# A causal mask added in two row-tiled bf16 products for each head

## The chip, the cores and the metric

The kernel runs on one core of one Trainium2 chip. The metric is the device time of one execution in microseconds; the figure for a kernel is the median of its runs. A profiled execution is shown beside it: its span reaches from the first to the last instruction, and its time is a little longer than its span.

## The reference

Three parts follow each other. Causal attention over batch 2, 12 heads, 448 positions, head width 64; then two dense layers with a smooth step between them; then a gated pair and its output layer.

```python
scores = scale * np.matmul(q, k.transpose(0, 1, 3, 2))     # 2 x 12 x 448 x 448
mask = np.triu(np.ones((seq, seq), dtype=bool), k=1)
scores = np.where(mask, -1000000000.0, scores)
scores = scores - np.max(scores, axis=-1, keepdims=True)
attn = np.exp(scores)
attn = attn / (np.sum(attn, axis=-1, keepdims=True) + 1e-09)
out = np.matmul(attn, v)                                    # then (896, 768)
...
h = x @ w_in                                                # (896, 2048)
g = np.where(h >= 1, h, np.where(h <= -1, 0.0, (h + 1) ** 2 / 4))
x = g @ w_out                                               # (896, 768)
...
g = x @ w_gate; val = x @ w_val                             # (896, 1536)
return (g / (1 + np.exp(-g)) * val) @ w_out2                # (896, 768)
```

## The kernel before, in words

Attention works on pairs of heads. A tile `qk_t` holds the transposed queries and keys of two heads, the first in partitions 0 to 63, the second in 64 to 127. The 896 tokens are handled in two groups of 448: group 0 is the first 224 positions of both batches, group 1 the last 224. There are 12 units (a batch and a pair of heads) in each group. A unit of group 0 is one step (`j == 0`, query blocks 0 and 1 of 112 rows each), a unit of group 1 is two steps (`j == 2` and `j == 3`, one query block each): 12 + 24 = 36 steps. `SEGS` says for each step which stretches of columns its scores have: 112 and 224 columns, or 336, or 448.

A step goes through the engines like this. `scores` puts the products of queries and keys into the PSUM tile `s`, one bank for each head (TensorE, line 249); each is fp32 and runs in two passes, and its operands are the 64 rows of one head. Behind it the same function adds the causal mask to the last 112 columns of each stretch, by a product of a bf16 identity with a bf16 mask, 112 rows each (line 255). `greatest` reduces to the row maximum (VectorE, lines 267 and 269), `exps` takes the exponential (ScalarE, line 281), `normalize` divides by the sum (VectorE, lines 292, 293, 305), `turn` transposes the weights (TensorE, line 316), `turned` copies them out of PSUM (ScalarE, line 325), and `values` multiplies with the values (TensorE, line 336 for group 0, 349 for group 1), whose outputs for the two heads stand in the two halves of the columns. `x_hi` and `x_lo` split the result for the next layer.

The steps are pipelined: one pass of the main loop holds the scores of step k + 1, the normalization of step k, the transposes of step k - 1 and the values of step k - 2, in an order that the lists in `ORDER` give. That order is what the program states; when it is built, a scheduler puts each engine's instructions in the order in which they are expected to be ready, the stated order deciding between those that are. So scores, transposes and values of neighbouring steps can be interleaved otherwise than stated.

Where TensorE would have nothing to do, the loop gives it filling work: up to the second step of group 1 products of zeros (`zeros`, line 370, bf16, 512 columns; 18 ahead of everything as a warm-up, then `HOLD` many in each step), later the products of the first dense layer (`h_products`, lines 70 to 72). The weights of that layer arrive meanwhile, and VectorE unpacks them (lines 108, 115, 119, 128). Nine of sixteen blocks of the layer are done for group 0 during attention; all else of the dense layers follows.

The constants are made at the start: `ident` by GpSimd, `mask_b` by a memset on VectorE (line 374) and a selection on GpSimd (line 378), `ident_b` by one copy on VectorE (line 382).

Of the kernel before, what the change touches and what calls it, by code (L numbers as in the profile page):

```python
# [8 lines left out]
F32 = mybir.dt.float32  # L9
# [4 lines left out]
ALU = mybir.AluOpType  # L14
# [3 lines left out]
B, H, S, D = 2, 12, 448, 64  # L18
# [3 lines left out]
C = 112  # L22
# [14 lines left out]
MASK = -1.0e9 * 8.0  # L37
BF16 = mybir.dt.bfloat16
LOW_V = 9
NORM_P = 0  # L40

ORDER = {
    0: "copy scores max fill values x_hi weights norm x_lo turn exp relu square g_hi g_lo".split(),
    2: "copy scores fill max relu values exp norm x_hi x_lo turn square g_hi g_lo weights".split(),
    3: "copy scores fill max relu values exp norm x_hi x_lo turn square g_hi g_lo weights".split(),
}
TURN0 = "A"
TURN1 = "A"
NORM0 = "V"
NORM1 = "V"  # L50
PINNED = 2
TICKS = (1, 0, 3)


# [1 line left out]
def fused_kernel(ctx: ExitStack, tc: tile.TileContext, qk, v, w_in, w_out, w_gv, w_o2, out):  # L56
    nc = tc.nc

    const = ctx.enter_context(tc.tile_pool(name="const", bufs=1))
    ident = const.tile([128, 128], F32, name="ident")  # L60
    ident_b = const.tile([128, C], BF16, name="ident_b")
    mask_b = const.tile([128, C], BF16, name="mask_b")
    half_b = const.tile([128, 1], F32, name="half_b")
    half_x = const.tile([128, 1], F32, name="half_x")
    xy = ctx.enter_context(tc.tile_pool(name="xy", bufs=2))
# [13 lines left out]
    class Weights:  # L79
# [20 lines left out]
        def operations(self):  # L100
            for i, (_, n) in enumerate(self.srcs):
# [9 lines left out]
                )  # L111
                if i < PINNED:
                    tc.keep_in_program_order(first)
# [102 lines left out]
    with ExitStack() as ph:  # L216
# [22 lines left out]
        def scores(k):  # L239

            u, j = steps[k]
            qk_t, _ = ld[u]
            s = ps_s.tile([128, 2, 512], F32, tag="s", name="s")
            k0 = GT if j == 0 else 0

            for i, (off, w, q0) in enumerate(reversed(SEGS[j])):
                for h in range(2):
                    hd = slice(h * D, (h + 1) * D)
                    nc.tensor.matmul(  # L249
                        out=s[:C, h, off:off + w], lhsT=qk_t[hd, q0:q0 + C], rhs=qk_t[hd, k0:k0 + w],  # L250
                        start=(i == 0), stop=False, skip_group_check=True,
                    )
            for off, w, _ in SEGS[j]:
                for h in range(2):
                    nc.tensor.matmul(  # L255
                        out=s[:C, h, off + w - C:off + w], lhsT=ident_b[:C, :], rhs=mask_b[:C, :],
                        start=False, stop=True, skip_group_check=True,
                    )
            st[k] = {"s": s}

        def greatest(k):
# [25 lines left out]
        def normalize(k):  # L287
# [6 lines left out]
            for i, (off, w, _) in enumerate(segs):  # L294
                if j == 0 and NORM_P:
                    nc.gpsimd.tensor_tensor(
# [3 lines left out]
                else:  # L300
                    norms = NORM0 if j == 0 else NORM1
                    for h in range(2):
# [16 lines left out]
        def turned(k):  # L319
# [3 lines left out]
            off, w = (336 if j == 3 else 0), NK[j] * C  # L323
            turns = TURN0 if j == 0 else TURN1
            (nc.vector.tensor_copy if turns[k % len(turns)] == "V" else nc.scalar.copy)(
# [42 lines left out]
        def zeros(n):  # L368
# [2 lines left out]

        zeros(WARM)
        make_identity(nc, ident)
        nc.vector.memset(mask_b, 0.0)
        nc.vector.memset(half_b, 0.5)

        nc.scalar.activation(out=half_x, in_=half_b, func=AF.Exp)
        nc.gpsimd.affine_select(
            out=mask_b[:C, :], in_=mask_b[:C, :], compare_op=ALU.is_ge, fill=MASK,
            base=0, pattern=[[-1, C]], channel_multiplier=1,  # L380
        )
        nc.vector.tensor_copy(out=ident_b, in_=ident[:, :C])
        fill, done, fresh = None, 0, []

        def filler():
# [16 lines left out]
        for k in range(-1, last + 2):  # L402
# [3 lines left out]
            for op in ORDER[kind]:  # L406
                if op == "copy" and lag:
                    turned(k - 2)
                elif op == "scores" and lead:
                    scores(k + 1)  # L410
                elif op == "max" and lead:
                    greatest(k + 1)
# [120 lines left out]
    for hf in range(2):  # L533
# [14 lines left out]
        for i in range(last):  # L548
            w = W.get(I_O2 + hf * NB + i)
# [52 lines left out]
```

## Time and profile before

| | |
|---|---|
| median of 3 runs | 623.25 us (623.1 to 624.42) |
| the profiled execution | 624.03 us, its span 622.2 us |
| instructions | 8660 |
| mean granted TensorE clock | 0.999 |

The page of the profile has one execution. Busy times are unions of an engine's instructions; matmuls overlap, and their ends are modelled, so the start of the next one tells more than a matmul's own duration. PE is TensorE's products, PEld its weight loads, DVE VectorE, ACT ScalarE, POOL GpSimd, SP SyncE. "L255" is line 255 of the kernel. A tile's name stands with its operation: `s` are scores, `t` transposes, `o` values, `mm` either products of the dense layers (L70 to L72) or products of zeros (L370).

### The profile page before, as it was taken

Reading aid. Unit: us, or ns where it says so; the run is one execution under the profiler, and the core shown is the slowest. Engines: PE = TensorE matmul, PEld = TensorE weight load, DVE = VectorE, ACT = ScalarE, POOL = GpSimd, SP = SyncE. Lnnn points to the kernel's source line nnn. Section 1 sums busy time; section 2 is a strip of 40 time slices with the busy share of each in tenths; the row PEclk is TensorE's granted clock in tenths of the full one; section 3 lists DMA queues with packets and bytes.
Section 4 is the critical chain, followed back from the end, with each engine's and each line's share of the span. In section 5 each row is a group of like instructions: output and inputs, shape, how many; then the busy total and the mean of one; then the engine's idle time right before and its main releaser. Section 6 shows DMA issues by size and latency. Waiting matters only on the chain.

```text
span 622.2 us, 8660 instructions
## 1 busy us (share of the span) xinstructions
PE 612.5 (98%) x3394; PEld 534.1 (86%) x3398; DVE 362.6 (58%) x687; ACT 210.4 (34%) x455; POOL 118.0 (19%) x68
## 2 busy tenths in 40 slices
PE   9999999998999999999999999999999999999997
PEld 4665666667999999999999999999999999999997
DVE  3899999964697766533435355655555555532401
ACT  2776776664434444121121222222222222112100
POOL 0000000000221222222222223222222223321300
PEclk9999999999999999999999999999999999999999
DMA  7565464300041233433343323333333333335002
GB/s 244 153 230 176 133 180 139 121 1 1 1 160 44 85 102 89 134 96 122 101 136 102 108 97 110 125 120 101 106 109 128 116 102 102 101 108 172 14 0 90
DMA packets 18665, 67.81 MB, mean 109 GB/s; under 512 B 2112, under 2 KB 6784, under 8 KB 18624
## 3 DMA queue, kind: packets, MB, share of 16 engines
q1 hardware_dynamic: 18624, 67.25, 34.2%
q8 instruction: 27, 0.44, 0.3%
q14 instruction: 14, 0.11, 0.1%
HBM read 64.49 MB, written 2.75 MB: 108 GB/s over the span
## 4 chain that ended last, share of the span: by engine, by line
PE 90%; DVE 5%; ACT 4%; issue 1%; ACTq 0%
PE mm L70 22%; PE mm L71 21%; PE mm L72 21%; PE mm L542 5%; PE mm L544 5%; PE mm L543 5%; PE s L249 3%; PE t L316 3%; ACT p L281 2%; PE mm L370 2%; PE o L349 2%; PE o L336 1%; DVE s L267 1%; DVE p L305 1%; PE s L255 1%
## 5 line engine op out<-in xcount | busy, mean ns | idle before, releaser
L128 POOL TENSOR_TENSOR wl<-wt,wh 128x768 fp32r<-128x768 f32 (+1 forms) x61 | 117.0, 1920 | 473.7 <-ACT wh L127 473.7
L127 ACT CAST wh<-wt 128x768 fp32r<-128x768 f32 (+1 forms) x70 | 57.4, 820 | 178.4 <-PE mm L71 108.4
L72 PE MATMUL mm<-yh,wl 128*128 128x448 f32 x288 | 105.2, 365 | 0.0
L71 PE MATMUL mm<-yl,wh 128*128 128x448 f32 x288 | 105.2, 365 | 0.0
L70 PE MATMUL mm<-yh,wh 128*128 128x448 f32 x288 | 105.2, 365 | 0.0
L108 DVE TENSOR_SCALAR wt<-wraw 128x768 int32<-128x768 int32 (+1 forms) x70 | 41.5, 593 | 108.9 <-POOL wl L128 108.8
L70 PE MATMUL mm<-xh,wh 128*128 128x448 f32 x192 | 72.5, 377 | 2.7 <-DVE q L192 2.7
L71 PE MATMUL mm<-xl,wh 128*128 128x448 f32 x192 | 70.1, 365 | 0.0
L70 PE MATMUL mm<-gh,wh 128*128 128x448 f32 x192 | 70.1, 365 | 0.0
L71 PE MATMUL mm<-gl,wh 128*128 128x448 f32 x192 | 70.1, 365 | 0.0
L72 PE MATMUL mm<-gh,wl 128*128 128x448 f32 x192 | 70.1, 365 | 0.0
L72 PE MATMUL mm<-xh,wl 128*128 128x448 f32 x192 | 70.0, 365 | 0.0
L115 DVE SCALAR_TENSOR_TENSOR wt<-wraw,wt 128x768 int32<-128x768 int32 (+1 forms) x70 | 67.6, 966 | 1.3
L119 DVE SCALAR_TENSOR_TENSOR wt<-wraw,wt 128x768 int32<-128x768 int32 (+1 forms) x70 | 65.2, 932 | 1.6
L72 PEld LDWEIGHTS mm<-yh,wl 128*128 128x128 f32 x288 | 54.1, 188 | 4.3
L71 PEld LDWEIGHTS mm<-yl,wh 128*128 128x128 f32 x288 | 54.1, 188 | 4.3
L70 PEld LDWEIGHTS mm<-yh,wh 128*128 128x128 f32 x288 | 54.1, 188 | 4.3
L544 PE MATMUL mm<-wh,ul 128*128 128x384 f32 x168 | 56.1, 334 | 0.0
L542 PE MATMUL mm<-wh,uh 128*128 128x384 f32 x168 | 56.1, 334 | 0.0
L543 PE MATMUL mm<-wl,uh 128*128 128x384 f32 x168 | 56.1, 334 | 0.0
L281 ACT ACTIVATE p<-s,mx 112x112 f32<-112x112 f32 (+3 forms) x96 | 46.5, 497 | 21.0 <-DVE mx L269 19.1
L70 PEld LDWEIGHTS mm<-xh,wh 128*128 128x128 f32 x192 | 36.1, 188 | 6.9 <-DVE q L192 3.5
(63 smaller groups left out, 827.8 us busy)
## 6 DMA issues: line engine op xcount, KB each, us to landing
wraw<-w_gv SPq DMA_DIRECT2D x24, 768.0 KB, 4.2
wraw<-w_in SPq DMA_DIRECT2D x16, 768.0 KB, 4.5
wraw<-w_out SPq DMA_DIRECT2D x12, 768.0 KB, 4.4
wraw<-w_o SPq DMA_DIRECT2D x12, 768.0 KB, 4.2
qk_t<-qk SPq DMA_DIRECT2D x12, 336.0 KB, 2.9
wraw<-w_out SPq DMA_DIRECT2D x6, 512.0 KB, 3.8
qk_t<-qk SPq DMA_DIRECT2D x12, 224.0 KB, 3.8
v_t<-v SPq DMA_DIRECT2D x12, 224.0 KB, 2.6
```

The costliest lines, as they stand in the source:

```text
L70: nc.tensor.matmul(out=ps, lhsT=wh, rhs=xh, start=first, stop=False)
L71: nc.tensor.matmul(out=ps, lhsT=wh, rhs=xl, start=False, stop=False)
L72: nc.tensor.matmul(out=ps, lhsT=wl, rhs=xh, start=False, stop=last)
L108: first = nc.vector.tensor_scalar(out=t, in0=w[:, :, 1], scalar1=3, scalar2=0x3FFFFFF8, op0=ALU.logical_shift_left, op1=ALU.bitwise_and,)
L115: nc.vector.scalar_tensor_tensor(out=t, in0=w[:, :, 1], scalar=-0x40000000, in1=t, op0=ALU.bitwise_and, op1=ALU.bitwise_or,)
L119: nc.vector.scalar_tensor_tensor(out=t, in0=w[:, :, 0], scalar=29, in1=t, op0=ALU.logical_shift_right, op1=ALU.bitwise_or,)
L127: nc.scalar.copy(out=wh[:, :n], in_=t.bitcast(F32))
L128: (nc.vector if i < LOW_V else nc.gpsimd).tensor_tensor(out=wl[:, :n], in0=t.bitcast(F32), in1=wh[:, :n].bitcast(F32), op=ALU.subtract,)
L281: nc.scalar.activation(out=p[:, h, off:off + w], in_=s[:C, h, off:off + w], func=AF.Exp, bias=mx[:, i, h:h + 1], scale=0.125, accum_out=sm ...
L542: nc.tensor.matmul(out=ps, lhsT=c, rhs=a, start=(f == 0), stop=False)
L543: nc.tensor.matmul(out=ps, lhsT=c, rhs=b, start=False, stop=False)
L544: nc.tensor.matmul(out=ps, lhsT=d, rhs=a, start=False, stop=(f == FC2 - 1))
```

## The change

The mask is added by two products for each head in place of one. Each uses the 64 partitions of its head: the first head's identity and mask rows are in partitions 0 to 63, the second's in 64 to 127, so that the products have the same rows of the array as the scores of that head. `ident_b` and `mask_b` become tiles of 128 x 2 x 112: index 0 holds rows 0 to 63 of the identity and the mask, index 1 the 48 rows that remain (as a slice of 64, whose last 16 are zero in the identity). They are filled by eight copies from an fp32 identity and an fp32 mask. A step of group 0 then has eight mask products instead of four, a step of group 1 four instead of two. Some constants move to other lines.

```diff
-    ident_b = const.tile([128, C], BF16, name="ident_b")
-    mask_b = const.tile([128, C], BF16, name="mask_b")
+
+    ident_b = const.tile([128, 2, C], BF16, name="ident_b")
+    mask_b = const.tile([128, 2, C], BF16, name="mask_b")
+    mask = const.tile([128, C], F32, name="mask")
...
             for off, w, _ in SEGS[j]:
-                for h in range(2):
-                    nc.tensor.matmul(
-                        out=s[:C, h, off + w - C:off + w], lhsT=ident_b[:C, :], rhs=mask_b[:C, :],
-                        start=False, stop=True, skip_group_check=True,
-                    )
+                for i in range(2):
+                    for h in range(2):
+                        hd = slice(h * D, (h + 1) * D)
+                        nc.tensor.matmul(
+                            out=s[:C, h, off + w - C:off + w], lhsT=ident_b[hd, i], rhs=mask_b[hd, i],
+                            start=False, stop=(i == 1), skip_group_check=True,
+                        )
...
-        nc.vector.memset(mask_b, 0.0)
+        nc.vector.memset(mask, 0.0)
...
         nc.gpsimd.affine_select(
-            out=mask_b[:C, :], in_=mask_b[:C, :], compare_op=ALU.is_ge, fill=MASK,
+            out=mask, in_=mask, compare_op=ALU.is_ge, fill=MASK,
             base=0, pattern=[[-1, C]], channel_multiplier=1,
         )
-        nc.vector.tensor_copy(out=ident_b, in_=ident[:, :C])
+        for i in range(2):
+            for h in range(2):
+                hd, rows = slice(h * D, (h + 1) * D), slice(i * D, (i + 1) * D)
+                nc.vector.tensor_copy(out=ident_b[hd, i], in_=ident[rows, :C])
+                nc.vector.tensor_copy(out=mask_b[hd, i], in_=mask[rows, :])
```

## Rows read from the trace of the kernel before

**Rows 1.** The page, busy us (share of the span) and instructions.

```profile
PE 612.5 (98%) x3394; PEld 534.1 (86%) x3398; DVE 362.6 (58%) x687; ACT 210.4 (34%) x455; POOL 118.0 (19%) x68
```

**Rows 2.** Table by stage: stretch, us, busy us (instructions), clock, DMA share and GB/s.

```profile
core 0: us, PE busy (x) PEld busy (x) DVE busy (x) ACT busy (x) POOL busy (x), PEclk, DMA share, GB/s
8.00:19.60 11.60, 10.85 (x85) 6.75 (x85) 7.15 (x28) 5.42 (x25) 0.00 (x0) 1.00 0.65 218
19.60:48.00 28.40, 27.99 (x241) 19.39 (x242) 27.56 (x91) 23.05 (x84) 0.00 (x0) 1.00 0.64 204
48.00:62.50 14.50, 14.50 (x91) 8.20 (x89) 13.38 (x41) 9.34 (x28) 0.00 (x0) 1.00 0.56 178
62.50:119.00 56.50, 54.75 (x372) 36.37 (x371) 54.15 (x133) 39.09 (x96) 0.00 (x0) 1.00 0.50 156
119.00:142.00 23.00, 22.30 (x156) 15.60 (x156) 16.21 (x45) 14.17 (x38) 0.00 (x0) 1.00 0.01 2
...
152.00:622.20 470.20, 466.62 (x2376) 438.51 (x2375) 239.15 (x342) 112.67 (x177) 117.05 (x61) 1.00 0.31 99
```

**Rows 3.** The chain that ended last: score products; start us, us, what.

```profile
41.56 0.76 PE s L249 x8
...
48.23 0.75 PE s L249 x4
...
52.96 0.74 PE s L249 x2
...
54.43 0.74 PE s L249 x2
```

**Rows 4.** The chain: mask products (L255).

```profile
42.32 0.34 PE s L255 x4
...
48.99 0.24 PE s L255 x2
...
55.89 0.10 PE s L255 x2
```

**Rows 5.** The chain: behind mask, zeros, values, values, mask, mask, scores, scores, in order.

```profile
34.32 0.22 PE mm L370
34.54 0.48 PE t L316 x5
...
37.47 0.32 PE mm L370
...
40.85 0.72 PE t L316 x6
...
46.11 0.26 PE mm L70
...
49.23 0.72 PE o L336 x8
...
53.71 0.72 PE o L336 x8
...
97.39 0.40 PE mm L70
```

**Rows 6.** Groups by line and shape: busy us, mean ns of one.

```profile
L249 PE MATMUL s<-qk_t 64*112 64x224 f32 x48 | 9.4, 393 | 0.3
```

**Rows 7.** Timeline of TensorE at 13.14 us: start us, us from first start to last end.

```profile
13.14 0.45 PE L249 MATMUL s<-qk_t 64*112 64x224 f32 x2
```

**Rows 8.** VectorE's waits from 8 to 152 us: total us, times, longest us.

```profile
DVE s L267 <- PE s L255: 9.3, 6, 7.9
```

**Rows 9.** Timeline of the start: start us, us, instruction, idle time before it.

```profile
1.26 0.28 POOL L378 TENSOR_SCALAR_AFFINE_SELECT mask_b<-mask_b 112x112 bf16<-112x112 bf16 x1
...
1.34 0.27 DVE L382 CAST ident_b<-ident 128x112 bf16<-128x112 f32 x1
...
9.11 0.41 PE L255 MATMUL s<-mask_b,ident_b 112*112 112x112 bf16 x4
...
9.56 1.49 DVE L267 TENSOR_REDUCE s<-s 112x2 f32<-112x224 f32 x3 [7.95 <-PE s L255]
```

More of the change, by code (lines that the diff above doesn't have):

```diff
@@ L40 @@
 NORM_P = 0
+TURN0 = "A"
+TURN1 = "A"
+NORM0 = "V"
+NORM1 = "V"
+PINNED = 2
 ORDER = {
@@ L46 @@
 }
[L47 to L51, printed above, removed]
 TICKS = (1, 0, 3)
```

## The prediction

> **What bounds the kernel now.** I began with the busy shares: TensorE is at 98% of the span and nothing else passes 60% [rows 1]. That is a mean over stages, so the table by stage came next [rows 2]. After 152 us TensorE works through 470 us of plain products that the change doesn't touch; whatever the attention part saves or loses arrives at the end unchanged. The attention part has four kinds of stretch: a start (8 to 19.6 us) in which all engines wait for one another; 19.6 to 62.5 us, where TensorE has no gap worth the name but VectorE is nearly full too (27.56 of 28.40 and 13.38 of 14.50 us); 62.5 to 119 us, where VectorE is busy for 54.15 of 56.50 us; and 119 to 142 us, where VectorE is down to 16.21 of 23 us and TensorE runs on.
>
> Then I followed the chain of work that ended last. It runs through TensorE alone from 19 to 28 and from 32 to 62 us and again from 119 to 140 us, and in between mostly through VectorE and ScalarE. Of the 36 groups of mask products (one group for each step) 19 lie on it: two in the start, ten between 20 and 62 us, two between 62.5 and 119 us, five after 119 us. Only there is a saving on TensorE worth anything. The remaining views say what such a group costs, and who waits for it.
>
> **What a mask group costs now.** In the chain a group of four takes 0.34 us and a group of two 0.24 us [rows 4]: (0.34 - 0.24)/2 = 0.05 us for a product, and 0.14 us beside it in either. One group has no such 0.14 us: two products in 0.10 us, and it is the one that follows transposes instead of scores [rows 4]. So the 0.14 us belongs to the passage from products on half the array's rows (scores) to products on 112 rows (mask). The same passage shows behind the mask when the rows change there: the warm-up product of zeros takes 0.22 us behind a mask group and 0.32 us behind values, an MLP product 0.26 us behind a mask and 0.40 us behind scores [rows 5]. The values, which use half the columns, take 0.72 us behind the mask and 0.72 us behind scores alike [rows 5]: they pay the passage either way. It isn't the type that costs: transposes (fp32) behind zeros (bf16) take 0.48 us for five, 0.10 each with nothing extra, while six behind values, fp32 both, take 0.72 us [rows 5].
>
> **What the change does to that.** (1) The passage between scores and mask goes: -0.14 us for each group behind scores. (2) It comes back behind the mask: +0.10 us before zeros, +0.14 us before an MLP product, nothing before values, which paid already.
>
> (3) The products: 96 become 192. Their price isn't in the trace, since no bf16 product on 64 rows is. Upper bound: all go one after the other at 0.05 us, so the 96 added ones cost 96 x 0.05 = 4.8 us of TensorE, of which 54 are on the chain (8 in the start, 24 in six groups of eight up to 46 us, then 8, 4 and 10), 2.7 us. Lower bound: the two heads run side by side, nothing added. A product on fewer rows can't take less than the 0.05 us, since as many columns stream, so no gain is possible here. I take the lower bound, because the nearest row is clear: two score products of different heads, 0.39 us each on the mean [rows 6], are both done within 0.45 us [rows 7].
>
> (4) The weight loads double as well. A step of group 0 has four score passes for each head, 2 x 224 + 2 x 112 = 672 columns, with four loads; a step of the first kind in group 1 has two passes of 336, also 672 columns, with two loads. They take 0.76 and 0.75 us [rows 3]. Twice the loads in the same half of the array cost 0.01 us: they hide behind the product before them. I take nothing for the loads. The Trainium skill says otherwise ("TensorE: Matmul & The Clock Gate", Part 3: a weight load overlaps a running matmul only where the row groups differ); by it every second product of a head would wait for its load and the group would be longer, which is the first rival's result. The rows just named disagree with it.
>
> (5) The mask is complete 0.14 us sooner after the scores, so VectorE's maximum can begin sooner. It waited for a mask six times, 9.3 us in all, of which 7.9 is the very first [rows 8]. The first counts in full: VectorE starts its reductions at 9.56 us, right behind the first group [rows 9], and the chain goes through them: -0.14 us. Of the five others (1.4 us together) three fall where the chain is TensorE's; I count none of them, and keep up to -0.3 us for the two behind 96 us as the other end.
>
> (6) The set-up: eight copies of 64 x 112 in place of one of 128 x 112, which takes 0.27 us [rows 9]; at most 8 x 0.27 - 0.27 = 1.9 us more on VectorE, and a mask selection of twice the bytes on GpSimd, which has nothing else to do. All stand behind the first memset and are done near 4 us; VectorE idles 7.95 us until 9.56 us [rows 9], and the first mask product is at 9.11 us. Nothing; without that cover it would be 1.9 us.
>
> **The sum**, with the order on TensorE as it is, over the 19 groups of the chain: the start -0.14; four groups followed by zeros (at 24.8, 34.0, 39.6 and 42.3 us) 4 x (-0.14 + 0.10) = -0.16; two followed by values (49.0 and 69.1 us) -0.28; the one at 55.9 us behind transposes now pays on both sides, +0.14 + 0.14 = +0.28; nine followed by MLP products, five of them after 119 us, 0; the one at 21.1 us, which is followed by an idle moment, 0; the second of the start, counted with the first, 0. Together -0.30 us. The profiled execution took 624.03 us (span 622.2 and 1.83 around it), 0.78 above the median of the runs. 624.03 - 0.30 = 623.73, so 622.95 beside the median of 623.25. I say 622.9. A measurement of this kernel can tell about 0.2%, 1.25 us, from no change, so this is no change. With (5) at its other end it is 622.6; if the group at 55.9 us stands elsewhere, another 0.3 either way.
>
> **Rivals.** *First, slower: the two heads don't share the time.* If a pair of products takes 0.10 us and not 0.05, whether because loads are exposed or because four instructions can't be issued in 0.05 us, the 54 products of the chain cost 2.7 us and the result is 622.95 + 2.7 = 625.65. It decides from about 0.03 us for each pair ((1.25 + 0.3)/54). For it: no row shows bf16 pairs, and the shortest pair of the scores is of longer passes. Against it: [rows 3, 6, 7].
>
> *Second, the order of TensorE's work changes.* It is worked out when the program is built, from when each operation is expected to be ready, and a mask that is eight instructions instead of four moves these moments. What the order is worth is seen in steps whose two heads were torn apart: 0.74 + 0.74 us, with other work between, where both heads together take 0.75 [rows 3]. Four such steps lie on the chain before 62 us, 4 x 0.73 = 2.9 us. If the new order keeps two of them together, that is -1.5 us, to 621.5; VectorE has 0.84 + 1.12 = 1.96 us of idle time between 19.6 and 62.5 us [rows 2], so no more than about 2 us can come of it. If it tears two or three more apart, +1.5 to +2.2 us, to 624.5 or 625.1. For it: up to 62 us the order differs from step to step. Against it: after 99 us it repeats, and the shifts are of 0.1 or 0.2 us.
>
> *Third, the change doesn't do what it says.* The array empties between scores and mask all the same, at the change from fp32 to bf16, and again behind the mask. Then the four groups before zeros cost +0.10 each, ten before MLP products +0.14 each (that at 55.9 us +0.28 in all), those before values nothing: 0.4 + 9 x 0.14 + 0.28 = 1.9 us, to 625.2. Against it: the transposes behind zeros [rows 5].
>
> **How the numbers follow.** The forecast as summed 0.48 (own range 622.2 to 623.6); the order better by 1.3 us or more 0.25, worse by as much 0.11; the heads one after the other 0.12; the third rival 0.04. Faster by over 0.2% is the better order and a little of the forecast's lower edge: 0.29. Slower is the three others, less what of them stays under 1.25 us: 0.24. Within 0.2%: 0.47. The range leaves out about one in ten on each side: down to 621.2, where a better order with the 0.3 us saved has come near the limit that VectorE sets; up to 625.4, which takes in the third rival and most of the first.
>
> **What would show it.** In the profile after, the chain's mask groups should take about 0.20 us (eight products) and 0.10 us (four), and the MLP product behind them 0.40 us instead of 0.26. Two mask products of different heads should start within some ns of each other. TensorE's matmul count should be 3394 + 96, VectorE's first reduction start near 9.42 us. A group of eight that lasts 0.4 us shows the first rival, 0.14 us left in front of the group the third; steps torn apart in other places than now show the second, and so does any change over 1 us with the groups as short as said. A first mask product later than 9.1 us would show that the set-up isn't hidden.

## The result, and the profile after

The changed kernel takes 629.22 us (median of 5 runs, 628.08 to 629.42) against 623.25 us: a ratio of 1.0086, 95% interval 1.0073 to 1.0099. It is slower by 6 us, just under 1%, where 0.3 us less was predicted, and outside the range. The profiled execution took 629.42 us, its span is 627.6 us: 5.4 us more than before.

The page's busy times after the change, and the table by stage in the stretches of [rows 2]:

```profile
PE 616.9 (98%) x3488; PEld 536.7 (86%) x3494; DVE 363.4 (58%) x694; ACT 210.2 (33%) x455; POOL 116.9 (19%) x68
```

```profile
8.00:19.60 11.60, 10.21 (x101) 6.67 (x103) 7.12 (x29) 5.52 (x26) 0.00 (x0) 1.00 0.64 220
19.60:48.00 28.40, 26.89 (x277) 18.66 (x280) 28.19 (x93) 23.43 (x85) 0.00 (x0) 1.00 0.70 216
48.00:62.50 14.50, 13.93 (x103) 8.99 (x102) 14.23 (x43) 11.20 (x32) 0.00 (x0) 1.00 0.56 174
62.50:119.00 56.50, 55.76 (x405) 39.75 (x402) 54.12 (x132) 37.94 (x93) 0.00 (x0) 1.00 0.47 151
119.00:142.00 23.00, 21.73 (x164) 15.96 (x160) 16.41 (x46) 14.70 (x37) 0.00 (x0) 1.00 0.00 1
152.00:622.20 470.20, 470.20 (x2356) 434.84 (x2355) 237.84 (x340) 112.05 (x176) 115.93 (x61) 1.00 0.31 98
```

TensorE has 94 more products on record; the change adds 96, and a few products are missing from either trace. But the surprise is in the last row: in the same 470.2 us after 152 us, TensorE finished 2356 products, where it finished 2376 before [rows 2], and those products are plain dense ones that the change doesn't touch. It was busy for all of the time, at the same granted clock (1.00); before, the stretch even holds the end of the kernel, 3.6 us without a product. So the loss is not in attention. The trace says so too: the last value product (the last product of attention) started at 148.78 us, 2.12 us sooner than before (150.90). From there to the end of the span it was 478.86 us instead of 471.31, which is 7.55 us more. -2.12 and +7.55 make the +5.4.

A narrow look at the dense part, first before and then after. 300 to 350 us is the second dense layer, 400 to 500 us the third (products that overlap an edge of the window count in full):

```profile
300.00:350.00 50.00, 50.00 (x249) 46.33 (x248) 20.81 (x28) 7.36 (x11) 12.26 (x8) 1.00 0.36 114
...
400.00:500.00 100.00, 100.00 (x495) 92.67 (x494) 57.24 (x83) 25.95 (x42) 29.29 (x14) 1.00 0.36 111
```

```profile
300.00:350.00 50.00, 50.00 (x244) 45.41 (x243) 20.29 (x28) 7.34 (x11) 13.07 (x8) 1.00 0.37 119
...
400.00:500.00 100.00, 100.00 (x486) 90.83 (x485) 57.65 (x83) 24.55 (x40) 29.69 (x14) 1.00 0.34 104
```

Nine products fewer in 100 us. From start to start, the mean over the 864 products of layer 3 in the trace is 202.67 ns before and 206.67 ns after, and the same over the 576 of layer 2. In the trace 1872 products of 448 columns start after the last value product (eight blocks of layer 1 are done by then, not nine): 1872 x 4.0 ns = 7.5 us, the whole loss to 0.1 us. The groups by line and shape show which products are hit, the first line before, the others after. The duration of one (365 ns before in the first group, 334 ns in the other) is modelled, but it moves the same way:

```profile
L70 PE MATMUL mm<-yh,wh 128*128 128x448 f32 x288 | 105.2, 365 | 0.0
...
L72 PE MATMUL mm<-yh,wh 128*128 128x448 f32 x288 | 106.0, 368 | 0.0
...
L551 PE MATMUL mm<-wh,uh 128*128 128x384 f32 x168 | 56.1, 334 | 0.0
```

The 384-column products of the last layer, which stream the weights, are at 173.34 ns from start to start in both.

What the change did to the others is a matter of place. The constants take 896 bytes more in each partition, and everything allocated behind them moves. In the built programs the streamed operands of the dense layers begin at byte 18432 instead of 17536 of a partition, the weights at 79872 instead of 78976. Before, both are at 128 modulo 256, after, both at 0. A place ("at 128") is always meant modulo 256 below.

The attention part did what was predicted, almost to the row. The chain that ended last, after, for a group of eight and one of four:

```profile
43.87 0.76 PE s L251 x8
44.63 0.20 PE s L260 x8
...
100.32 0.75 PE s L251 x4
101.08 0.10 PE s L260 x4
101.18 0.40 PE mm L72
```

Eight mask products take 0.20 us and four 0.10, with no passage in front (0.34 and 0.24 before [rows 4]), and the dense product behind takes 0.40 us instead of 0.26 [rows 5]. Two mask products of different heads start 6 or 7 ns apart in the trace, and a pair starts 49 to 52 ns after the pair ahead of it: the heads share the time, and the doubled weight loads cost nothing, as step (4) had it. On the loads the rows again disagree with one rule of the Trainium skill ("TensorE: Matmul & The Clock Gate", Part 3), that a load overlaps running products only where the row groups differ; the same part also lets a load into the background weight buffer go ahead, and with that the rows are in keeping. On the two heads they agree with its small start difference (about 4 ns there).

VectorE's waits for the mask fell from 9.3 to 7.5 us [rows 8], but its first reduction came later, not sooner:

```profile
DVE s L272 <- PE s L260: 7.5, 3, 6.8
```

```profile
9.78 0.41 DVE s L272
```

It stood at 9.56 us before [rows 9]; the first score product was at 7.98 and is at 8.08 us, so 1.58 us after it before and 1.70 now. More of the second unit's scores had come between. The first mask product is at 9.13 us, past the 9.1 us that the prediction named as the sign of a set-up that isn't hidden. It isn't that sign here: the eight copies had ended by 3 us, the first score product came 0.10 us later, and the mask followed it after 1.04 us instead of 1.13. TensorE's order is another one, and the experiments below put most of the 2.1 us down to it.

### The profile page after: what moved, and what is told of

The parts are those of the page before. It is cut to its first block, busy times and chain, and to the rows that moved or that the text cites. A ratio compares the mean times of both kernels' runs of the same rounds, so it can differ in the third digit from the quotient of the medians.

```text
span 627.6 us, 8847 instructions
## 1 busy us (share of the span) xinstructions
PE 616.9 (98%) x3488; PEld 536.7 (86%) x3494; DVE 363.4 (58%) x694; ACT 210.2 (33%) x455; POOL 116.9 (19%) x68
## 4 chain that ended last, share of the span: by engine, by line
PE 94%; DVE 2%; ACT 2%; issue 0%; ACTq 0%
PE mm L72 23%; PE mm L73 22%; PE mm L74 22%; PE mm L551 5%; PE mm L553 5%; PE mm L552 5%; PE s L251 4%; PE t L321 3%; PE o L354 3%; PE mm L375 2%; ACT p L286 1%; PE o L341 1%; DVE s L272 1%; ACT pt L330 1%; PE s L260 1%; DVE p L310 0%
## 5 line engine op out<-in xcount | busy, mean ns | idle before, releaser
L72 PE MATMUL mm<-yh,wh 128*128 128x448 f32 x288 | 106.0, 368 | 0.0
L72 PE MATMUL mm<-xh,wh 128*128 128x448 f32 x192 | 73.3, 382 | 2.3 <-DVE q L194 2.3
L72 PE MATMUL mm<-gh,wh 128*128 128x448 f32 x192 | 70.7, 368 | 0.0
L72 PEld LDWEIGHTS mm<-yh,wh 128*128 128x128 f32 x288 | 54.1, 188 | 5.6
L72 PEld LDWEIGHTS mm<-xh,wh 128*128 128x128 f32 x192 | 36.0, 188 | 8.4 <-DVE q L194 4.4
```

The source lines that it names most:

```text
L72: nc.tensor.matmul(out=ps, lhsT=wh, rhs=xh, start=first, stop=False)
```

## The experiments

Three things are mixed in the result: the price of the mask products, the order of the attention work, and the places of what lies behind the constants. A time called "attention" below is from the first score product to the start of the last value product in the trace (142.92 us before, 140.70 after); it leaves out when the first load lands, which moves the whole by up to 1.6 us from one execution to another. It is read from one profiled execution of each kernel. Ten of the changed kernel, whose versions differ only in unused bytes and their filling, took 140.31 to 140.74 us, and four of the kernel before 142.83 to 143.00 us, so a difference of 0.3 us between two of them is of the size of their scatter.

### The places

**128 bytes more behind the constants of the changed kernel.** A tile of one number takes 32 bytes; 40 numbers take 128 more.

```diff
-    half_x = const.tile([128, 1], F32, name="half_x")
+    half_x = const.tile([128, 40], F32, name="half_x")
...
-        nc.scalar.activation(out=half_x, in_=half_b, func=AF.Exp)
+        nc.scalar.activation(out=half_x[:, :1], in_=half_b, func=AF.Exp)
```

> The changed kernel with 128 unused bytes more per partition behind its constants, nothing else. Theory 1 (place): the larger constants moved every later tile by 896 bytes, and the 448-column products of the dense layers take 0.2067 us from start to start there instead of 0.2027 us; a start that is an odd multiple of 128 bytes again brings back 0.2027 us, and 629.2 becomes about 621.8 us, below the kernel before. Theory 2 (the longer stream of TensorE's instructions, or anything else of the mask products, slows the dense layers): 0.2067 us and 629.2 us stay.

621.01 us (620.29 to 622.26), ratio 0.9962 (0.9949 to 0.9975): 8 us less than the changed kernel, and faster than the kernel before. Layers 2 and 3 are back at 202.67 ns.

**The opposite: the kernel before with 896 unused bytes** (the same edit, 232 numbers).

```diff
-    half_x = const.tile([128, 1], F32, name="half_x")
+    half_x = const.tile([128, 232], F32, name="half_x")
```

> The kernel before with 896 unused bytes more per partition behind its constants, so that all later tiles stand where the changed kernel has them; no other edit. Theory 1 (place): the 448-column products of the dense layers go from 0.2027 to 0.2067 us, some 1850 of them, and 623.25 becomes about 630.7 us. Theory 2 (instructions): 0.2027 us and 623.25 us stay.

631.05 us (630.35 to 631.56), ratio 1.0119 (1.0102 to 1.0136): the loss without the change, at 206.67 ns in layers 2 and 3. The stretch 400 to 500 us, of the changed kernel with 128 bytes and of the kernel before with 896:

```profile
400.00:500.00 100.00, 100.00 (x496) 92.68 (x495) 56.39 (x83) 25.26 (x41) 29.33 (x14) 1.00 0.35 111
```

```profile
400.00:500.00 100.00, 100.00 (x485) 90.83 (x485) 56.26 (x81) 25.57 (x41) 29.81 (x14) 1.00 0.34 103
```

**64 bytes in the kernel before** (24 numbers), to see whether any shift hurts.

```diff
-    half_x = const.tile([128, 1], F32, name="half_x")
+    half_x = const.tile([128, 24], F32, name="half_x")
```

> The kernel before with 64 unused bytes more per partition behind its constants. Theory 1 (place): the 448-column product changes from 0.2027 us to some value between 0.200 and 0.207 us (which one is open; the step of 64 bytes tells whether only multiples of 128 count). Theory 2: 0.2027 us and 623.25 us stay.

624.5 us in a single execution, 202.67 ns in both layers: for these two it doesn't.

**Operands and weights moved apart.** In the changed kernel, first 128 bytes between the operands' pool and the weights' (operands at 0, weights at 128), then 128 behind the constants and 1920 between (operands at 128, weights at 0):

```diff
+    gap = ctx.enter_context(tc.tile_pool(name="gap", bufs=1)).tile([128, 32], F32, name="gap")
     wp = ctx.enter_context(tc.tile_pool(name="wp", bufs=WBUFS))
...
+        nc.vector.memset(gap, 0.0)
```

> The changed kernel with a gap of 128 unused bytes behind the activations of the first and third dense layers, so that these stay on multiples of 256 bytes while weights, and the second layer's activations, stand 128 bytes past such a multiple. If the place of the streamed operand decides: 0.2067 us for a product in the first and third layer, 0.2027 us in the second. If the place of the weights decides: 0.2027 us in all three, 621 us. If the distance of the two decides (0 modulo 256 in all kernels so far): something else in the first and third layer, perhaps 0.200 us.

622.41 us in a single execution, like the next five runs: 202.69 ns in layer 2 (whose operands `gh`, `gl` lie behind the weights, at 128 here), 204.0 in layer 3.

```diff
-    half_x = const.tile([128, 1], F32, name="half_x")
+    half_x = const.tile([128, 40], F32, name="half_x")
...
+    gap = ctx.enter_context(tc.tile_pool(name="gap", bufs=1)).tile([128, 480], F32, name="gap")
```

> The changed kernel with the opposite split: the activations of the first and third dense layers 128 bytes past a multiple of 256, weights and the second layer's activations on multiples of 256. If the streamed operand decides: 0.2027 us in the first and third layer, 0.2067 us in the second. If the weights decide: 0.2067 us in all three, 629 us. If the distance decides: the first and third layer as in the run with the other split.

625.84 us: 206.65 ns in layer 2 (all at 0), 204.0 in layer 3. So the place of the streamed operand and that of the weights both count: one of them at 0 costs 1.33 ns, a third of the loss, and both 4.0.

**Other places**, by the same two edits: 24 numbers (all at 64), 56 numbers (all at 192), and 40 numbers with a gap of 16 or 24 numbers (operands at 128, weights at 192 or 224).

```diff
-    half_x = const.tile([128, 1], F32, name="half_x")
+    half_x = const.tile([128, 24], F32, name="half_x")
```

> The changed kernel with 64 unused bytes behind the constants: the 448-column operands of the dense layers and their weights begin at 64 mod 256. Theory C, only the place 0 mod 256 is bad (places of 128 and of 192 gave 202.67 ns for a product): 202.7 ns, and about 621 us. Theory D, the cost grows towards 0: between 202.7 and 206.7 ns, 622 to 628 us.

> The changed kernel with 192 unused bytes behind the constants: operands and weights both at 192 mod 256 in layers 1 to 3, as in the kernel before with 64 bytes (202.67 ns). If the places alone set the rate: 202.67 ns, about 621.5 us. If it also hangs on something else in the kernel: 206.5 ns as in layer 2 of the kernel with a gap of 64 bytes, 626 us or more.

621.93 and 621.87 us, 202.67 ns: of four shifts tried with operands and weights at one place (0, 64, 128, 192), only 0 costs in layers 2 and 3.

```diff
+    gap = ctx.enter_context(tc.tile_pool(name="gap", bufs=1)).tile([128, 16], F32, name="gap")
```

> The changed kernel with 128 unused bytes behind the constants and 64 between the operands and the weights: operands at 128, weights at 192 mod 256. If any place other than 0 mod 256 is as good as another, 202.7 ns for a product and about 621 us; if it is the distance of the two places that counts (64 here), another rate than 202.7, in either direction, 618 to 625 us.

> The changed kernel with 128 unused bytes behind the constants and 96 between the operands and the weights: operands at 128, weights at 224 mod 256. In the first dense layer of the kernel before a stretch of products at 200 ns each had just these two places. If the places alone set the rate: about 200 ns for a product in layers 1 to 3, some 4 to 5 us under the kernel with 128 bytes alone, 616 to 617 us. If not: 202.7 to 204 ns and 621 to 623.5 us.

With 16 numbers 622.02 us: 202.22 ns in layer 3, but 206.66 in layer 2, whose operands and weights are both at 192, a place that gave 202.67 twice. With 24 numbers 617.3 us: layer 3 at 200.03 ns, layer 2, with both at 224, at 202.67 ns. The same stretch of that kernel:

```profile
400.00:500.00 100.00, 100.00 (x502) 93.84 (x501) 57.70 (x84) 26.14 (x42) 30.56 (x14) 1.00 0.35 108
```

**Operands at 128 and weights at 224 in all three layers**, in the changed kernel (40 numbers, a gap of 24, and one of 40 ahead of layer 2's operands) and in the kernel before (both gaps alone).

```diff
+    gap = ctx.enter_context(tc.tile_pool(name="gap", bufs=1)).tile([128, 24], F32, name="gap")
     wp = ctx.enter_context(tc.tile_pool(name="wp", bufs=WBUFS))
     ev = ctx.enter_context(tc.tile_pool(name="ev", bufs=2))
+    gap2 = ctx.enter_context(tc.tile_pool(name="gap2", bufs=1)).tile([128, 40], F32, name="gap2")
```

> The changed kernel with unused bytes so that the streamed operands of layers 1 to 3 begin at 128 and their weights at 224 mod 256. If the places alone set the rate: 200.0 ns for a 448-column product in all three layers, as in layer 3 of the kernel that had them there only; layer 2 is then 2.67 ns x 576 = 1.5 us shorter than in that one, about 615.8 us. If not: layer 2 between 202 and 207 ns, 617 to 620 us.

> The kernel before with the same places, and its own order of the attention work. If the places alone set the rate: 200.0 ns in all three layers and about 2.05 ns x 392 + 2.67 ns x 1440 = 4.6 us under the kernel before, 618.6 us. The changed kernel at the same places is then 2.4 us ahead (2.1 of it the order, 0.3 the mask). If not: 202 to 207 ns, 621 to 629 us.

> The same kernel as the one with operands at 128 and weights at 224 mod 256 in layers 1 to 3, for a second profiled execution. If the 617.5 us of its other executions come from a mixture of rates: some layers at 200.0 ns and a stretch of some 300 products at 206.67 ns (300 x 6.67 ns = 2 us over the 615.8 us that were expected). If the rest of the time lies elsewhere: 200.0 ns in all three layers, and 1.7 us more in front of them or behind.

The changed kernel had a ratio of 0.9902 (0.9887 to 0.9917), from three executions of 617.24 to 618.43 us; the kernel before 0.9945 (0.9932 to 0.9959), five of 619.52 to 621.01. But the profiled execution of each, which the ratios leave out, took 630.82 and 632.56 us, and a second one of the changed kernel 630.23 us. In the records of all three, layers 2 and 3 ran at 206.67 ns, layer 1 at about 207, and the 384-column products at 176.67. The changed kernel:

```profile
400.00:500.00 100.00, 100.00 (x486) 90.48 (x485) 57.86 (x83) 24.32 (x40) 29.45 (x14) 1.00 0.34 105
```

So the places alone don't set the rate: one kernel, with every operand where it was, ran either way. All three profiled executions of these kernels were long and none of the eight others was, so from their times the profiling itself can't be ruled out as the cause. But layer 1 shows both rates in profiled executions: five of its blocks have their weights in the pool `stay`, at 224 in every kernel, with operands at 128 in the kernel before. These 90 products ran at 200.0 ns in the kernel before and at 206.7 ns in two others with the same places (the next section's first two). Whether the 617.5 us hold a mixture of rates, as one expectation had it, stays open, for no such execution was profiled.

### The order of the attention work

**Eight products, full rows.** The kernel before, each mask product issued twice on its 112 rows (the mask is added twice): only the instructions' number changes.

```diff
-                for h in range(2):
-                    nc.tensor.matmul(
-                        out=s[:C, h, off + w - C:off + w], lhsT=ident_b[:C, :], rhs=mask_b[:C, :],
-                        start=False, stop=True, skip_group_check=True,
-                    )
+                for i in range(2):
+                    for h in range(2):
+                        nc.tensor.matmul(
+                            out=s[:C, h, off + w - C:off + w], lhsT=ident_b[:C, :], rhs=mask_b[:C, :],
+                            start=False, stop=(i == 1), skip_group_check=True,
+                        )
```

> The kernel before with each mask product issued twice, on 112 rows as before (the mask is added twice): as many products as the changed kernel, without half-array products and without larger constants. For the dense layers, theory 1 (place) says 0.2027 us for a product, theory 2 (instructions) 0.2067 us. For attention, theory A (the order on TensorE, which the count of products changes) says that scores and masks come in about the order of the changed kernel and that attention gains, less the 54 added products of the chain at 0.05 us = 2.7 us: about 0.5 us later than before instead of 2.2 us earlier. Theory B (the gain came from the half-array products themselves) says 2.7 us later.

626.74 us in a single execution; attention 144.90 us, 202.67 ns in layers 2 and 3. TensorE's order became nearly that of the changed kernel, so the number of products is enough to turn it; but without row halves they cost more than the order gives. Neither theory had the size: attention ends 1.98 us later than before, where they said 0.5 and 2.7 us.

**The kernel before in the changed kernel's order.** Edges without a wait tie each product of the attention part to the one that stands ahead of it in that order (the first two steps stay as before; `PE_ORDER` lists kinds and counts; s is a score, m a mask, z zeros, t a transpose, o a value, p a dense product).

```diff
+    seen = {t: [] for t in "zsmtop"}
...
+        left, prev = {t: iter(x) for t, x in seen.items()}, None
+        for word in PE_ORDER.split():
+            for _ in range(int(word[1:])):
+                ins = next(left[word[0]]).ins
+                if prev is not None:
+                    tc.add_manual_dep(ins, prev.name, info, reason="PE_ORDER")
+                prev = ins
```

> The kernel before, its mask products on 112 rows and its constants as they are, with TensorE's attention work forced into the order of the changed kernel (the first two steps as before). Theory A (order): attention ends about 1.9 us earlier than in the kernel before and the time is about 621.7 us. Theory B (half-array products): 623.6 us, no gain.

621.39 us (620.28 to 622.35), ratio 0.9962 (0.9949 to 0.9974); attention 140.76 us. With not one instruction of the change, the order alone is worth 2.15 us of attention; the orders of the other engines were left to the scheduler. It doesn't come evenly: counted from the first score product, the transposes of a step are 3.0 us ahead after 47 us, 1.5 us after 59 to 72 us, and 2.15 us at the end. The five `stay` blocks of layer 1 give 0.6 us of it back, 90 products x 6.7 ns.

**The changed kernel in the order of before** (128 bytes added): by TensorE's order alone (the same edit), and then with the orders of VectorE, ScalarE and the DMA queue as well:

> The changed kernel with 128 unused bytes more per partition (dense layers at 0.2027 us for a product, as in the kernel before) and with TensorE's attention work forced into the order of the kernel before: scores, masks, transposes, values, zeros and dense products as there, each mask product replaced by its two. Theory A (the attention gain of 2.2 us is the new order): only the sum of the prediction is left, -0.3 us, so about 623.3 us beside 623.6 for the kernel before. Theory B (the gain comes from the half-array products whatever the order): attention ends about 2.2 us earlier, 621.4 us.

625.11 us, ratio 1.0027 (1.0017 to 1.0038); attention 144.87 us. Neither the 0.3 us less that the prediction's sum asked for nor any loss that the mask's rows explain. The other engines had orders of their own: 261 of VectorE's 683 instructions and 76 of ScalarE's 356 stood elsewhere than before. (In the second edit `log` holds each engine's instructions as the program states them.)

```diff
+    for name, order in (("vector", VECTOR_ORDER), ("scalar", SCALAR_ORDER), ("sync", SYNC_ORDER)):
+        prev = None
+        for word in order.split():
+            a, _, b = word.partition(":")
+            for n in range(int(a), int(b or int(a) + 1)):
+                ins = log[name][n]
+                if prev is not None:
+                    tc.add_manual_dep(ins, prev.name, pinned, reason="ORDER")
+                prev = ins
```

> The changed kernel with 128 unused bytes behind the constants, and with the instructions of TensorE, VectorE, ScalarE and the DMA queue all in the order that they have in the kernel before (the mask's extra products stand where the mask's products stood). Forced into TensorE's order alone it was 1.5 us slower than before, not 0.3 us faster. Theory A, the prediction's sum is right and that loss came from the other engines' order, which then fitted TensorE's no longer: the time from the first score to the start of the last value product is about 142.6 us (142.92 before), and the median about 0.3 us under that of the kernel before. Theory B, the pairs of mask products themselves lose time in this order of TensorE's work: about 144.9 us for the attention, and 1.5 us slower than before.

623.34 us (622.27 to 624.36, 11 runs), ratio 0.9995 (0.9986 to 1.0004); attention 142.63 us, 0.29 less than before: the prediction's -0.30, with the order as it was. The first reduction starts 1.45 us behind the first score product instead of 1.58, 0.13 sooner where 0.14 was worked out:

```profile
6.58 1.01 PE L278 MATMUL s<-qk_t 64*112 64x224 f32 x9
...
8.03 1.06 DVE L71 TENSOR_REDUCE s<-s 112x2 f32<-112x224 f32 x2 [5.06 <-PE s L287]
```

The one group that should lose, behind transposes at 55.9 us, in the chain of before and of this kernel (the mask is L255 and L287, the dense product behind it L72 and L101):

```profile
55.89 0.10 PE s L255 x2
55.99 0.27 PE mm L72
```

```profile
54.05 0.24 PE s L287 x4
54.28 0.40 PE mm L101
```

0.37 us became 0.64: +0.27, worked out as +0.28.

The terms up to there hold in sum, those behind it only because two misses cancel. Counted from the first score product, the transposes ahead of this group start 0.44 us sooner than before, and those behind it 0.18 us; the prediction's terms make 0.44 and 0.16. Then the group followed by values at 69.1 us, put at -0.14, brings nothing (still 0.16 us, 100 us after the first score product; from 62.5 to 119 us VectorE is busy for 54.07 of 56.50 us). The last steps, put at nothing, bring 0.13. That the total comes so near to the sum is luck.

The 2.2 us that the kernel forced by TensorE's order alone lost in attention go to how the engines' orders fit each other; which of theirs it was wasn't tried.

## Why the prediction was wrong

The times by order of the attention work and by mask, dense layers 2 and 3 at 202.67 ns in all four:

| | order of before | order of the changed kernel |
|---|---|---|
| one product on 112 rows | 623.25 us (attention 142.92) | 621.39 us (140.76) |
| two products on row halves | 623.34 us (142.63) | 621.01 us (140.44) |

Down a column is what the prediction summed: -0.29 and -0.32 us of attention, each of the size of the scatter between single executions. Along a row is what the scheduler added: -2.15 and -2.19, far beyond that. The 0.6 us that the `stay` blocks of layer 1 give back stand in the times of the right column, not in its attention.

**The step that failed** is in "What bounds the kernel now": "After 152 us TensorE works through 470 us of plain products that the change doesn't touch; whatever the attention part saves or loses arrives at the end unchanged". The instructions were untouched, but their operands were moved. Step (6) of the change costed the constants by the time it takes to fill them and by nothing else; that `ident_b`, `mask_b` and `mask` stand ahead of every other allocation, in the diff's first lines, was read and not followed. It cost 7.5 us, 25 times the sum, and shows in both directions. From the last value product to the end of the span it is 471.3 us before and 478.9 after; 128 bytes more bring it to 471.9 (the `stay` blocks are the rest), and 896 unused bytes in the kernel before, without the change, to 478.7. No rival held it.

**The steps that held.** The passage (1) and (2), the heads side by side (3), the loads (4) and, where the order is that of before, the first reduction (5); the set-up is hidden (6): the eight copies end by 3 us and VectorE then idles 6.8 us for the mask. Of the sum's terms the one at 69.1 us did not hold, and the last steps made up for it. Of the views named ahead, the groups of 0.20 and 0.10 us and the 0.40 us behind them came as said. The first reduction near 9.42 us did not, since the order had changed.

**The second rival** happened beside the forecast, whose sum went by "the order on TensorE as it is": the order turned for the better. I gave it 0.25 and 1.5 us, with about 2 us as the most; it was 2.15, so the limit from VectorE's idle time was a little too low. One step that was torn in two [rows 3, at 52.96 and 54.43 us] runs together after, with its scores in one piece on the chain; how much of the 2.15 us comes from such steps was not taken apart.

```profile
53.17 0.75 PE s L251 x4
53.92 0.10 PE s L260 x4
```

Had the constants ended 128 bytes further on, the change would have shown 621.0 us, about that rival's 621.5, and below the range by 0.2 us. The first and the third rival are refuted by the groups' own lengths.

**What stays open** is why a place costs. Within one execution layers 2 and 3 each keep one rhythm from start to start: 207, 207, 206 at the bad place; about 199, 207, 202, 203, 202 where the mean is 202.67; 196, 203, 212, 200, 209 with one of the two at 0; at the best 200 throughout. And the place is not all: both at 192 gave 202.67 ns twice and 206.66 once, both at 0 gave 202.7 in three blocks of layer 1 of the kernel before with 896 bytes, and 128 with 224 went either way. What else takes part, no trace here shows.

## What to carry to other kernels

A new constant moves everything that is allocated behind it. Before a diff is costed, list which operands of untouched work change their place, and keep them where they were by a pad or by allocating the new tile last; after a run, compare the start-to-start time of products that the change doesn't touch. And where a scheduler sets the order, force the old order once on all engines: it separates what an edit costs from what the order does with it, which was here seven times as much.

Of the versions tried the changed kernel with 128 unused bytes is the one to keep: 0.9962 of the time before, with all five runs below every run of the kernel before. Nearly all of that is the order, for the kernel before reached the same ratio in it. The version with the weights at 224 reached 0.9902, but the same kernel also took over 630 us.

## What was not expected of the hardware

The rate of products of 448 columns with a weight load under each (operands of type F32R, which the profile prints as f32) goes with where in a partition the streamed operand and the weights begin. From start to start, in layers 2 and 3, it was 202.67 ns with both at 64, 128 or 192 modulo 256 (but once 206.66 with both at 192), 204.0 with one of them at 0, 206.67 with both, and with 128 and 224 it was 200.0 in one profiled execution and 206.67 in three. At the same granted clock (1.00) and with TensorE busy throughout, this is 3% of a dense layer. The Trainium skill says that loading the next weights does not take read bandwidth from the running product ("TensorE: Matmul & The Clock Gate", Part 2, Step-by-step: what each phase is for); here the weights' place alone, with the operand's unchanged at 128, made 202.67 into 204.0 ns, while the loads' own mean duration stayed at 188 ns. So the weights' place does reach the rate of the products; whether by the reads, no run here shows.
